# A gated attention and GEGLU kernel: wider staging, down weights split twice, late weight writes, attention in two stages

## The chip, the cores and the metric

The kernel runs on one core of a Trainium2 chip. The core has five engines that run in parallel, each through its own list of instructions in order: PE (TensorE, matrix products into PSUM banks), ACT (ScalarE), DVE (VectorE), POOL (GpSimd) and SP (SyncE, which here only issues DMAs). They meet at semaphores. DMAs are issued from the queues of SP, ACT and POOL. The metric is the device time of one execution in microseconds, and a kernel's figure is the median of its runs.

## The reference

For x of 2048 tokens and 512 channels, all in float32:

```
g   = sigmoid((x * gate_w).sum(-1))
a   = attention(x @ wqkv) @ wo      # 32 heads of 16 channels; a token sees itself and 7 earlier
                                    # ones at a distance of 2, 4, ... 14; softmax over these 8
b   = (gelu(x @ w_gate) * (x @ w_up)) @ w_down      # 1792 hidden channels
out = g * a + (1 - g) * b
```

Attention has a dilation of 2, so even tokens see even tokens alone, and odd ones odd ones alone.

## The kernel before, in words

**Precision.** A float32 factor is made into two parts of a type that PE multiplies at once: hi is the rounded value, lo the rest. A product is hi·hi + hi·lo + lo·hi, three matmuls of 128 x 128 by 128 x 512. Parts are made by `split` (L78): ACT copies hi, DVE subtracts to get lo. For the weights of the FFN another way is used: ACT writes the negated rounded value into the place of lo (scale -1), and a DMA from POOL's queue that adds (`accum_op`) puts the raw value on top; then ACT writes hi. That is one adding DMA and two ACT passes for each group.

**Order.** `par` is 0 for the 1024 even tokens, 1 for the odd ones; each is 8 tiles of 128 tokens (`jj`), in two blocks of 4. The order as written (L660 on) is: projection of even tokens, FFN 0 (even tokens), projection of odd tokens, attention output of even tokens (`finish(0)`), FFN 1 (odd tokens), attention output of odd tokens (`finish(1)`). The order as run is made at compile time by a scheduler with its own timing of each instruction; it keeps dependences and mixes the rest by priority, engine by engine. It also hands out tiles: a name such as "s" or "r" has a fixed number of buffers, and an instruction that wants one waits until the last user of that buffer is done. Every DMA issued by SP or ACT takes one of eight semaphores in turn, and waits on its queue until the DMA that had it before (eight places earlier) has landed; POOL's DMAs have eight of their own.

**Projections.** `project(par, cb)` makes keys and queries of half of the heads (cb 0 and 2) or values and the gate (cb 1). For each tile, 12 matmuls go to a PSUM bank (L179), and `take` (L185) copies it with ACT into a stage tile (L191) and stores it to HBM with two DMAs from ACT's queue (L194, L196). Stage tiles come from "s" (3 buffers) and "r" (2 buffers) in turn. The buffers "hh" and "hl" (6 each) hold parts elsewhere.

**Attention.** It is DVE's work. A unit is 128 channels (8 heads) of one parity; there are 8 units. `load_kq` loads k and q from HBM, `scores` multiplies and sums (L246, L248), `softmax` takes the maximum (L258), subtracts it (L260), lets ACT take exp (L262), sums (L263) and scales; `mix` loads v, multiplies and adds (L281 to L289), transposes and stores to HBM from SP's queue ("os", L296). `attention()` is a generator that yields after each few instructions; `pull` advances it from within projections and FFN, at a lower priority, so DVE does it between other work.

**FFN.** The 1792 hidden channels come in 14 chunks f. The gate and up weights of a chunk are fetched (`fetch`, POOL's queue), combined on DVE (`combine`, L360), and split into parts in two groups, g0 and g1 (`operands`, L365; two buffers each). `gate_up` makes gate and up for both blocks of tokens by a scheme of seven products in place of eight, each of 6 matmuls (L411), in three banks X_, W_ and Z_: after the first product b11, ACT copies X_ to W_ (L490); t1 into Z_, copied to p5 (L415); t2 into X_, copied to u2; a12 b21 into W_ gives the gate of block 0, and so on. The seventh product of f is issued within f + 1 (`fourth`). Gate goes through gelu (L506, L523), is multiplied by up (L424) and split (L426, L427; lo on DVE in FFN 0, on POOL in FFN 1). `down` (L439) multiplies the hidden part of two chunks by the down weights, two chunks after they are made; block 0 is kept in four banks, block 1 goes through tiles "rt" (L444, L463).

**Weights for the second FFN.** In FFN 0, `keep(f)` (L387) writes the finished parts of g0 and g1 (768 and 1024 KB) to HBM ("ws") and those of the down weights d (512 KB, "ds"), from SP's queue, as soon as they are made. In FFN 1 `operands` and `down_w` (L396) load them from there. In FFN 0 `down_w` makes d from the raw down weights, fetched to a tile "r" by `fetch_d` (POOL's queue).

**Attention output.** `finish(par)` loads the attention's result back ("os"), splits it (`channels`, L605), multiplies by wo into eight banks (L638), copies each bank to a stage tile (L650 on ACT, L648 on DVE; "s" and "r" for even tokens) and stores or adds it to out (L652, L654).

Of the kernel before, what the change touches and what calls it, by code (L numbers as in the profile page):

```python
# [15 lines left out]
P = 128  # L16
# [24 lines left out]
def tile_gated_mix(ctx: ExitStack, tc: tile.TileContext, xt, wqkv, wff, wo, out):  # L41
# [44 lines left out]
    KS, VS, QS, OS, WS, DS = {}, {}, {}, {}, {}, {}  # L86
# [84 lines left out]
    stages = iter(["s", "r", "s", "r", "s"] * 99)  # L171
# [13 lines left out]
    def take(ps, par, jj, hh, vals, eng=None):  # L185
        st = tl(next(stages))
        n = CU if vals else 512
        if eng:
            eng.tensor_copy(st[:, :n], ps[:, :n])
        else:  # L190
            nc.scalar.activation(st[:, :n], ps[:, :n], AF.Copy)  # L191
        two = st.rearrange("p (a c d) -> p a c d", a=2, c=2)
        dst = VS[par, hh] if vals else KS[par, hh]
        nc.scalar.dma_start(rows(dst[:, W:], jj), two[:, 0])  # L194
        if not vals:
            nc.scalar.dma_start(rows(QS[par, hh], jj), two[:, 1])  # L196
        elif not hh:
            nc.scalar.activation(z[:, par, jj:jj + 1], ps[:, CU:CU + 1], AF.Copy)

    def project(par, cb, bg=iter(())):  # L200
        for jj in range(NP):
# [9 lines left out]
            next(bg, None)  # L211
            pull(2.7)
# [9 lines left out]
    LG = {}  # L222
# [30 lines left out]

    def softmax(par, u):
        lg = LG[par, u]
        m = pool.tile([P, NP, UH], F32, name="m")
        by_w = lg.rearrange("p j w h -> p j h w")
        nc.vector.tensor_reduce(m, by_w, axis=AX.X, op=OP.max)  # L258
        yield 0.7
        nc.vector.tensor_tensor(lg, lg, m[:, :, None, :].to_broadcast([P, NP, W, UH]), op=OP.subtract)  # L260
        yield 0.7
        nc.scalar.activation(lg, lg, AF.Exp, scale=DH ** -0.5)  # L262
        nc.vector.tensor_reduce(m, by_w, axis=AX.X, op=OP.add)  # L263
        yield 0.7
        nc.vector.reciprocal(m, m)
        nc.vector.tensor_tensor(m, m, g[:, par, :, None].to_broadcast([P, NP, UH]), op=OP.mult)
        yield 0.4
# [38 lines left out]
    def attention():  # L306
        units = [(0, u) for u in range(NU)] + [(1, u) for u in range(NU)]
        yield from need(0, 0)
        load_kq(0, 0)
        yield from scores(0, 0)  # L310
        load_kq(0, 1)
        yield from scores(0, 1)
        yield from need(0, 1)
        for i, un in enumerate(units):
            if i > 1:
                yield from scores(*un)
            yield from softmax(*un)
            if 1 <= i < len(units) - 1:
                yield from need(units[i + 1][0], units[i + 1][1] // 2 * 2)
                load_kq(*units[i + 1])  # L320
            yield from mix(*un)
            done.add((*un, "o"))

# [19 lines left out]
    RAW, RD, KEEP = {}, {}, {}  # L343
# [43 lines left out]
    def keep(f):  # L387

        for i in range(2):
            w = KEEP.pop((f, i))  # L390
            WS[f, i] = dram.tile(list(w.shape), F32, name=f"ws{f}{i}")
            nc.sync.dma_start(WS[f, i], w.bitcast(F32))
        DS[f] = dram.tile([P, 1024], F32, name=f"ds{f}")
        nc.sync.dma_start(DS[f], WD[f].bitcast(F32))

    def down_w(par, f):  # L396
        d = WD[f] = tl("d", F32R)
        if par:
            nc.sync.dma_start(d.bitcast(F32), DS[f])
            return  # L400
# [3 lines left out]
        nc.scalar.activation(d[:, :512], rd, AF.Copy)  # L404

    def product(ps, a, w, start):
        for kc in range(2):
            ah, al = XOP[a, kc]
            wh, wl = (x[:, kc * P:(kc + 1) * P] for x in w)
            for n, (w_, a_) in enumerate(((wh, ah), (wh, al), (wl, ah))):  # L410
                nc.tensor.matmul(ps, w_, a_, start=(start and kc == 0 and n == 0), stop=(kc == 1 and n == 2), skip_group_check=True)  # L411
# [54 lines left out]
    def gate_up(par, f, steps):  # L466
# [23 lines left out]
        nc.scalar.activation(W_, X_, AF.Copy)  # L490
        Z_ = bank("p")
# [12 lines left out]
        product(W_, "a12", w["b21"], False)  # L504
# [31 lines left out]
    def ffn(par):  # L536
        XOP.update(((n, kc), X[par, blk, kc + k]) for n, blk, k in (("a11", 0, 0), ("a12", 0, 2), ("a22", 1, 2))
                   for kc in range(2))
        for f in range(FC):
            def more():  # L540
                if f + 1 < FC:
                    for i, _ in enumerate(operands(par, f + 1)):
                        if i == 1 and not par and f + 2 < FC:
                            fetch(f + 2)
                        if i == 2 and not par:
# [4 lines left out]
                if f + 1 == FC and not par:  # L550
                    yield from before()
                if not par:
# [7 lines left out]
            down_w(par, f)  # L560
# [53 lines left out]
    def need_o(par, u):  # L614
        pull(1e9, (par, u, "o"))

    def finish(par, oT, bg):
# [6 lines left out]
        for u in range(NU):  # L624
# [7 lines left out]
            for jj in range(NP) if u + 1 < NU else [*range(BT, NP), *range(BT)]:  # L632
# [12 lines left out]
                r = tl(("s", "rt" if par else "r")[jj % 2])  # L645
# [64 lines left out]
    project(1, 2)  # L710
    finish(0, {}, iter(()))
# [44 lines left out]
```

## Time and profile before

| what | value |
|---|---|
| median of 3 runs | 663.26 us (662.86 to 665.01) |
| the profiled execution | 665.45 us |
| its span, first to last instruction | 663.6 us |
| its mean granted PE clock | 0.984 of full speed |
| PE busy | 623.3 us, 94% |
| DVE busy | 518.5 us, 78% |
| ACT busy | 338.8 us, 51% |
| POOL busy | 136.1 us, 21% |
| bytes moved by DMA | 153.97 MB |

The profile names an instruction by its line, its engine and the tiles that it writes and reads. A row of PE counts matmuls; each is shown for about 0.4 us, but they overlap, so the time of a row of matmuls that follow each other is read from its start to the next row's start. "x <- y" in a list of waits says which engine sat idle and what released it. A q after an engine's name (SPq, ACTq) stands for its queue, where DMAs are issued. In a table of stretches the columns are the stretch, its length, PE's busy time with the number of matmuls, the granted clock, the busy share of the DMA engines, and GB/s. A row of the chain gives start, length and what the end of the kernel waited for at that time. Rows of DMA issues give the count, the size and the median time from issue to landing.

### The profile page before, as it was taken

The page shows a single profiled execution, that of the slowest core. Times are in us where ns is not written, and L with a number is a line of the kernel's source. Part 1 is how long each engine was busy: PE and PEld are TensorE (multiplying, and loading weights), DVE is VectorE, ACT ScalarE, POOL GpSimd, SP SyncE. Part 2 cuts the span into 40 slices and gives each one's busy share as a digit, 9 for nine tenths or more (in the row PEclk, how much of TensorE's full clock was granted, in tenths as well). Part 3 has the DMA queues.
Part 4 walks back from the last instruction along what each step waited for, and adds up shares of the span by engine and source line. Part 5 has one row for each costly group of instructions (what it writes and reads, how often), then busy time and mean ns, then how long its engine had stood idle before and what let it go on. Part 6 is the DMA issues. An engine that isn't in the chain of part 4 may idle for free.

```text
span 663.6 us, 8115 instructions
## 1 busy us (share of the span) xinstructions
PE 623.3 (94%) x2839; PEld 507.0 (76%) x2839; DVE 518.5 (78%) x567; ACT 338.8 (51%) x581; POOL 136.1 (21%) x161
## 2 busy tenths in 40 slices
PE   8999569998999998988999999799999999999997
PEld 7898447777778786776889888588878888878885
DVE  6939179988799789697984798988998999981241
ACT  5535057574667856558655422234445435444561
POOL 5012013132223222121110001342212222021100
PEclk9999979999999999998999999799999999999999
DMA  8688969999999999995669997954757472543113
GB/s 257 184 248 219 361 191 234 334 315 286 329 303 314 269 365 251 323 268 200 191 199 318 309 330 208 218 179 165 269 190 269 149 258 112 179 142 124 38 58 126
DMA packets 75336, 153.97 MB, mean 232 GB/s; under 512 B 7712, under 2 KB 43168, under 8 KB 71712
## 3 DMA queue, kind: packets, MB, share of 16 engines
q1 hardware_dynamic: 36000, 103.84, 43.9%
q0 software_dynamic: 13184, 37.04, 23.5%
q10 hardware_dynamic: 26112, 12.59, 6.5%
q8 instruction: 22, 0.36, 0.2%
q14 instruction: 18, 0.15, 0.1%
HBM read 80.76 MB, written 56.16 MB: 206 GB/s over the span
## 4 chain that ended last, share of the span: by engine, by line
PE 49%; DMA 26%; DVE 9%; issue 8%; ACT 5%; POOL 2%; ACTq 1%; SPq 0%; POOLq 0%; DVEq 0%
PE p L411 18%; DMA g<-raw 10%; PE p L179 7%; PE acc L179 7%; PE p L450 6%; PE acc L450 5%; PE p L638 3%; PE acc L638 3%; DMA raw<-wff 2%; DMA vs<-s 2%; DMA qs<-s 2%; DMA q<-qs 2%; DMA raw<-xt 2%; DVE prod L281 2%; DMA ws<-g 1%
## 5 line engine op out<-in xcount | busy, mean ns | idle before, releaser
L411 PE MATMUL p<-S,g 128*128 128x512 f32 x672 | 174.1, 400 | 18.9 <-ACT r L191 12.0
L411 PEld LDWEIGHTS p<-S,g 128*128 128x128 f32 x672 | 127.6, 191 | 51.6 <-ACT r L191 12.5
L411 PE MATMUL p<-A,g 128*128 128x512 f32 x504 | 133.4, 399 | 10.2 <-DMA g<-raw 6.2
L411 PEld LDWEIGHTS p<-A,g 128*128 128x128 f32 x504 | 95.0, 190 | 36.4 <-DMA g<-raw 9.4
L246 DVE TENSOR_TENSOR prod<-k,q 128x2048 f32<-128x2048 f32 x32 | 73.0, 2280 | 9.2 <-DMA q<-qs 9.0
L427 POOL TENSOR_TENSOR hl<-c,hh 128x512 fp32r<-128x512 f32 x28 | 45.4, 1622 | 160.4 <-ACT hh L426 117.1
L281 DVE TENSOR_TENSOR prod<-v,lg 128x2048 f32<-128x2048 f32 x32 | 75.0, 2343 | 0.8 <-DMA v<-vs 0.2
L450 PE MATMUL p<-d,hh 128*128 128x512 f32 x224 | 70.0, 401 | 4.9 <-ACT p L444 4.9
L248 DVE TENSOR_REDUCE lg<-prod 128x128 f32<-128x2048 f32 x32 | 73.0, 2281 | 0.3
L450 PE MATMUL acc<-d,hh 128*128 128x512 f32 x224 | 59.1, 395 | 0.0
L450 PEld LDWEIGHTS p<-d,hh 128*128 128x128 f32 x224 | 42.5, 191 | 16.3 <-ACT p L444 6.7
L426 ACT ACTIVATE hh<-c 128x512 fp32r<-128x512 f32 x56 | 35.2, 628 | 34.5 <-DVE c L424 34.1
L424 DVE TENSOR_TENSOR c<-c 128x512 f32<-128x512 f32 x56 | 38.4, 685 | 14.7 <-ACT c L523 14.1
L450 PEld LDWEIGHTS acc<-d,hh 128*128 128x128 f32 x224 | 42.0, 188 | 9.9 <-ACT hh L426 0.3
L463 ACT ACTIVATE rt<-p 128x512 f32<-128x512 f32 x48 | 28.0, 592 | 42.2 <-PE p L450 42.1
L420 DVE TENSOR_TENSOR c<-p,s 128x512 f32<-128x512 f32 x56 | 38.1, 682 | 13.5 <-PE p L411 13.1
L415 ACT ACTIVATE s<-p 128x512 f32<-128x512 f32 x56 | 32.8, 592 | 26.2 <-PE p L411 19.1
L450 PE MATMUL p<-d,hl 128*128 128x512 f32 x112 | 43.3, 401 | 0.0
L285 DVE TENSOR_TENSOR prod<-prod 128x1024 f32<-128x1024 f32 x32 | 39.5, 1235 | 0.3
L381 POOL DMA_DIRECT2D g<-raw x28 | 26.9, 1009 | 37.4 <-ACT g L380 32.3
L360 DVE TENSOR_TENSOR raw<-raw 128x256 f32<-128x256 f32 (+1 forms) x42 | 21.2, 507 | 16.9 <-DMA raw<-wff 11.6
L380 ACT ACTIVATE g<-raw 128x1024 fp32r<-128x1024 f32 (+1 forms) x28 | 26.6, 950 | 15.3 <-DVE raw L360 12.7
(150 smaller groups left out, 975.1 us busy)
## 6 DMA issues: line engine op xcount, KB each, us to landing
ws<-g SPq DMA_DIRECT2D x14, 1024.0 KB, 7.8
g<-ws SPq DMA_DIRECT2D x14, 1024.0 KB, 5.2
ws<-g SPq DMA_DIRECT2D x14, 768.0 KB, 8.6
g<-ws SPq DMA_DIRECT2D x14, 768.0 KB, 5.8
raw<-wff POOLq DMA_DIRECT2D x28, 256.0 KB, 8.1
g<-raw POOLq DMA_DIRECT2D x14, 512.0 KB, 10.8
ds<-d SPq DMA_DIRECT2D x14, 512.0 KB, 7.7
d<-ds SPq DMA_DIRECT2D x14, 512.0 KB, 6.0
```

Of the source, the lines that this page charges most:

```text
L179: nc.tensor.matmul(ps[:, :cn], a[:, t], w[:, c0:c0 + cn], start=(kc == 0 and n == 0), stop=(kc == KC - 1 and n == 2))
L246: nc.vector.tensor_tensor(prod, spans(k, jj), q[:, jj:jj + 2, None, :].to_broadcast([P, 2, W, UC]), op=OP.mult)
L248: nc.vector.tensor_reduce(lg[:, jj:jj + 2].rearrange("p j w h -> p (j w h)"), prod.rearrange("p j w (h d) -> p (j w h) d", d=DH), axis=AX. ...
L281: nc.vector.tensor_tensor(prod.rearrange("p j w (h d) -> p j w h d", d=DH), spans(v, jj).rearrange("p j w (h d) -> p j w h d", d=DH), lg[: ...
L285: nc.vector.tensor_tensor(prod[:, :, :4], prod[:, :, :4], prod[:, :, 4:], op=OP.add)
L411: nc.tensor.matmul(ps, w_, a_, start=(start and kc == 0 and n == 0), stop=(kc == 1 and n == 2), skip_group_check=True)
L420: nc.vector.tensor_tensor(c, ps, s, op=OP.add)
L424: nc.vector.tensor_tensor(ge, ge, up, op=OP.mult)
L426: nc.scalar.activation(hh_, ge, AF.Copy)
L427: eng.tensor_tensor(hl_, ge, hh_.bitcast(F32), op=OP.subtract)
L450: nc.tensor.matmul(pp, a[:, ts], w, start=(i == 0 and n == 0 and gr == 0), stop=(i == 1 and n == 2), skip_group_check=True)
L638: nc.tensor.matmul(pa, a, b, start=(not par and u == 0 and n == 0), stop=(u == NU - 1 and n == 2), skip_group_check=True)
```

## The change

Five edits go together.

1. The stage tiles of projections go round "s", "hh", "hl", "hh", "hl" in place of "s", "r" (15 buffers in place of 5). The attention output of even tokens is staged in "hh" and "hl" in place of "s" and "r".
2. The parts of the down weights are no longer written to HBM and read back. `down_w` makes them in both FFNs, from raw weights that `fetch_d` loads in both. It is called in the background work of a chunk; `fetch_d(0)` for FFN 1 comes after the last projection.
3. The writes "ws" of chunk f get an added wait: for the last matmul of the product a12 b21 of that chunk.
4. Attention is split into two stages. Of a unit, scores, maximum and subtraction come one unit ahead of sum, scaling and mix, and the load of the next unit's k and q comes between scores and maximum. The tile m has two buffers.
5. Exp is taken out of the generator: a list holds the units that wait for it, and `exps` issues them on ACT at fixed places (after a projection tile, after the copy X_ to W_ of a chunk, or when a result is needed), after having been passed over a number of times, and in the order as written.

```diff
-    stages = iter(["s", "r", "s", "r", "s"] * 99)
+    stages = iter(["s", "hh", "hl", "hh", "hl"] * 99)
...
     def take(ps, par, jj, hh, vals, eng=None):
-        st = tl(next(stages))
+        st = tl(next(stages))[:, :512]
...
             next(bg, None)
+            exps(5)
             pull(2.7)
...
+    def below_max(par, u):
+        lg = LG[par, u]
+        m = M[par, u] = pool.tile([P, NP, UH], F32, name="m", bufs=2)
+        nc.vector.tensor_reduce(m, lg.rearrange("p j w h -> p j h w"), axis=AX.X, op=OP.max)
+        yield 1.2
+        nc.vector.tensor_tensor(lg, lg, m[:, :, None, :].to_broadcast([P, NP, W, UH]), op=OP.subtract)
+        EXPS.append([lg, 0, (par, u)])
+        yield 0.7
+
+    def exps(n=-1):
+
+        for e in list(EXPS):
+            e[1] += 1
+            if e[1] > n:
+                EXPS.remove(e)
+                tc.keep_in_program_order(nc.scalar.activation(e[0], e[0], AF.Exp, scale=DH ** -0.5))
+                done.add((*e[2], "e"))
+
     def softmax(par, u):
-        lg = LG[par, u]
-        m = pool.tile([P, NP, UH], F32, name="m")
...
-        nc.scalar.activation(lg, lg, AF.Exp, scale=DH ** -0.5)
...
+        yield from need(par, u, "e")
+        lg, m = LG[par, u], M.pop((par, u))
...
     def attention():
-        units = [(0, u) for u in range(NU)] + [(1, u) for u in range(NU)]
...
+        def start(i):
+            if i < len(units):
+                yield from scores(*units[i])
+                if i + 1 != NU:
+                    yield from load(i + 1)
+                yield from below_max(*units[i])
+
+        yield from load(0)
+        yield from start(0)
         for i, un in enumerate(units):
-            if i > 1:
-                yield from scores(*un)
+            if i + 1 != NU:
+                yield from start(i + 1)
+            yield from need(un[0], 1)
             yield from softmax(*un)
...
             yield from mix(*un)
             done.add((*un, "o"))
+            if i + 1 == NU:
+                yield from load(NU)
+                yield from start(NU)
...
             WS[f, i] = dram.tile(list(w.shape), F32, name=f"ws{f}{i}")
-            nc.sync.dma_start(WS[f, i], w.bitcast(F32))
-        DS[f] = dram.tile([P, 1024], F32, name=f"ds{f}")
-        nc.sync.dma_start(DS[f], WD[f].bitcast(F32))
-
-    def down_w(par, f):
+            gate(nc.sync.dma_start(WS[f, i], w.bitcast(F32)), MARK[f])
+
+    def down_w(f):
         d = WD[f] = tl("d", F32R)
-        if par:
-            nc.sync.dma_start(d.bitcast(F32), DS[f])
-            return
         rd = RD.pop(f)
         nc.scalar.activation(d[:, 512:], rd, AF.Copy, scale=-1.0)
         nc.gpsimd.dma_start(d[:, 512:].bitcast(F32), rd, accum_op=OP.add)
         nc.scalar.activation(d[:, :512], rd, AF.Copy)
+
+    def gate(ins, other):
+
+        tc.add_manual_dep(ins.ins, other.ins.name, mybir.DependencyInfo(mybir.DependencyClass.Sync,
+                          mybir.DependencyReason.SCHED_ONLY), reason="pace")
...
         nc.scalar.activation(W_, X_, AF.Copy)
+        exps(1)
...
-        product(W_, "a12", w["b21"], False)
+        MARK[f] = product(W_, "a12", w["b21"], False)
...
-                        if i == 2 and not par:
+                        if i == (0 if par else 2):
                             fetch_d(f + 1)
...
                 if f + 1 == FC and not par:
                     yield from before()
+                down_w(f)
+                yield
                 if not par:
                     keep(f)
...
-            down_w(par, f)
...
     def need_o(par, u):
-        pull(1e9, (par, u, "o"))
+        while (par, u, "o") not in done:
+            exps()
+            pull(1e9, (par, u, "o"))
...
-                r = tl(("s", "rt" if par else "r")[jj % 2])
+                r = tl((("s", "rt") if par else ("hh", "hl"))[jj % 2])[:, :512]
...
     project(1, 2)
+    fetch_d(0)
     finish(0, {}, iter(()))
```

## The prediction, made before the run

> **What bounds the kernel now.** I read the page's engine shares and 40 slices first, then TensorE (PE) over five stretches, then what PE waited for, then the chain and ScalarE's (ACT's) timeline where the largest gap lies, and the DMA issues last.
>
> ```profile
> PE 623.3 (94%) x2839; PEld 507.0 (76%) x2839; DVE 518.5 (78%) x567; ACT 338.8 (51%) x581; POOL 136.1 (21%) x161
> PEclk9999979999999999998999999799999999999999
> DMA  8688969999999999995669997954757472543113
> GB/s 257 184 248 219 361 191 234 334 315 286 329 303 314 269 365 251 323 268 200 191 199 318 309 330 208 218 179 165 269 190 269 149 258 112 179 142 124 38 58 126
> ```
> ```profile
> core 0: us, PE busy (x), PEclk, DMA share, GB/s
> 74.30:116.90 42.60, 27.82 (x109) 0.88 0.86 252
> 116.90:321.50 204.60, 190.94 (x803) 0.99 0.94 290
> 321.50:413.70 92.20, 92.20 (x494) 1.00 0.85 272
> 413.70:431.00 17.30, 12.95 (x44) 0.81 0.94 213
> 431.00:637.00 206.00, 204.76 (x882) 1.00 0.49 171
> ```
> ```profile
> PE p L411 <- ACT r L191: 12.0, 1, 12.0
> PE p L411 <- DMA g<-raw: 6.2, 6, 1.7
> PE p L411 <- ACT s L415: 5.2, 3, 3.4
> PE p L450 <- ACT p L444: 4.9, 3, 2.3
> PE p L411 <- DVE c L420: 3.9, 3, 1.6
> ```
> ```profile
> 62.40 7.73 DMA ws<-g
> 70.15 15.16 DMA qs<-s
> 100.47 5.06 DMA d<-r
> 105.53 2.88 DMA r<-wff
> 108.41 7.99 DMA g<-raw
> 461.60 5.59 PE p L411 x24
> ```
> ```profile
> 70.62 0.60 ACT L191 ACTIVATE r<-acc 128x512 f32<-128x512 f32 x1 [4.93 <-DMA ws<-g]
> 81.41 0.60 ACT L191 ACTIVATE s<-acc 128x512 f32<-128x512 f32 x1 [10.19 <-DMA qs<-s]
> 425.41 2.93 PE L411 MATMUL p<-S,g 128*128 128x512 f32 x6 [3.42 <-ACT s L415]
> ```
> ```profile
> ws<-g SPq DMA_DIRECT2D x14, 768.0 KB, 8.6
> ```
>
> What to see. PE is the bound: the chain has 24 matmuls in 5.59 us, 0.233 us each. A chunk f of the hidden channels needs 42 product and 24 down matmuls, 66 x 0.233 = 15.4 us. Length minus matmuls x 0.233 gives what each stretch loses: 17.2, 17.5, none (its matmuls are partly narrower, PE is busy throughout), 7.0 and 0.5; together 42.2. No part of this change removes a matmul, so these losses are all that it can win.
>
> The first loss is the end of the attention projections. ACT copies a projection to SBUF and issues its store to HBM itself. In the program every DMA of SyncE (SP) or ACT waits for the one eight places before it, since they share eight semaphores. So ACT's stores stood behind the weight writes ws and the v, k and q loads: one store was in flight for 15.16 us, and ACT waited 4.93 and 10.19 us while PE stood 12.0. The second loss is FFN 0 with DMA engines 94% busy. The third, at 413.7, is a copy that wants a stage tile "s" while the store of the attention output still holds it.
>
> **The change, part by part.** The sum is made against the profiled execution: 665.45 us, span 663.6 and 1.85 outside, 2.19 above the median of 663.26.
>
> A, projections and start of FFN 0 (74.3 to 116.9, loses 17.2). The rotation of stage tiles grows from 5 buffers to 15, and writes ws of f = 0 wait for that chunk's product a12 b21, about 81 us. Three writes (2.9 MB) that went out at 49.1, 62.4 and 64.9 leave this stage. Not all lanes clear: v, k and q loads of unit 0 and 1 still take places among the eight, and ACT's stores of tiles 4 to 6 wait for k and q (median 6.9 and 7.5 us; they can go out about 65, when DVE has left the old k). They end about 73 to 75, in time for the last projection at 74.3. So the 12.0 goes. What is late next is a chain on down weights. The new order puts both parts of d for f = 0 and 1 (whose loads now go first on POOL's queue, at the very start) before the chunk, and d for f = 2 and 3, ahead of the copy u2 of chunk 0, on ACT. Their loads wait on POOL for the d accumulations to land. From about 75.5: accumulation 5.8 (lowest of 14, median 7.9), issue 0.5, load 4.3 (row at 95.24; lowest 3.4, median 7.3), three ACT passes 1.9, copy 0.6: 88.6. PE can run 36 matmuls without u2, to 74.3 + 8.4 = 82.7, so it stands 6; with the lowest values 4, with the medians 11. Behind the same chain stands, on POOL, the accumulation of the first g weights of f = 2 (two loads ahead of it wait for d to land, 5.8 more): issued about 95.5, landing 8.0 later (row at 108.41) at 103.5, wanted at 100: 3.5, between 0 and 7. With 1.5 of slow clock (six matmuls at 0.42 after the old gap) the stage loses 11 in place of 17.2: minus 6. Ends: 4 left (minus 13), 17 left (nothing).
> By the Trainium skill (DMA: Bandwidth & Descriptors, Anatomy of one DMA) one transfer takes 2.0 us plus bytes / 436e3, 2.6 for these 256 KB; that is an estimate, and by it the chain would end under 82.7, nothing would stand there, and the sum would be 6 lower. The trace has 7.9 and 7.3 as medians, so I don't take it.
>
> B, FFN 0 (204.6 us, 803 / 66 = 12.2 chunks of 16.8). The writes ds leave: 14 x 0.524 MB. SP's queue moved 103.84 MB in 43.9% of the span, 2.8 us of all engines per MB, so 20.6 us; the three moved writes bring back 8.1. Net 12.5, about 1.0 per chunk. DMA work per chunk falls from 0.94 x 16.8 = 15.8 to 14.8, under PE's 15.4, so the six waits on g<-raw (6.2) should fall to 2. The 4.9 behind ACT L444 and 2.7 of the 3.9 behind DVE L420 stay, they are queue orders. Against it: writing late makes a loop. Product a12 b21 of f lets SP write both groups (SP also has attention's os stores and loads in that queue, which now wait behind the gated writes); ACT's first pass over the next g of the same buffer waits for the landing, and stands ahead of the copy W_ for chunk f + 1, without which the next a12 b21 can't run. Price of a round: landing L, lo and hi 1.7, hh, rt and W_ 1.8, every second round four d passes of 2.5, product 1.4: L + 6.2 on the mean. With the median 8.4 (4.2 to 19.0) this is 14.6, just under 15.4; six of 28 writes took over 11.4. I put 1 on it: 17.5 - 4.2 + 1 = 14; half of the DVE waits going with DVE's 17 us of exp wait moved earlier, I take 12.5. Minus 5, between minus 12.5 (5 left, the small waits alone) and plus 6.5 (24 left).
>
> C, output of even tokens (loses 7.0). Its stage tiles become hh and hl, so 3.42 and the slow clock behind it (2.93 for six matmuls, 1.5 too many, and four more at 0.42, 0.8) go: 5.7. ACT now has two d pairs and their loads ahead of the last attention channels; from 391 that chain takes 10 to 18, and PE wants them at 408: nothing to 3. I take 0.7. Minus 5 (minus 6.5 to minus 1).
>
> D, FFN 1 (loses 0.5). 28 ACT passes of 0.62 are 17.4 us on an engine about half busy, 28 POOL issues 22 us on one that is idle most of the time, and the reads of ds (7.3 MB) leave a DMA half idle. A d pair ahead of W_ costs 1.2 where PE is closely fed. Since d is used two chunks later, I take 0.5; 0 to 4.
>
> E, start. Two loads of 256 KB now go first, beside the x and w loads that PE waits for. The first slice moved 257 GB/s, so 0.52 MB costs up to 2.0. I take 1.
>
> F, at nothing: attention in two stages. DVE's waits for exp were 22.4, of which 17.0 is the wait of A; DVE is not PE's limit where attention runs out (its last units end about 40 us before FFN 1 does, and A to C take back about 15 of that). Exp now has a fixed place on ACT; its table loads stay 16 in the program. The projections of odd tokens lose nothing before, so more tiles bring nothing.
>
> Sum: -6 - 5 - 5 + 0.5 + 1 = -14.5; 665.45 - 14.5 = 650.95 as a profiled execution, less 2.19: **649**.
>
> **Rivals.** (1) Chains at unloaded latency: fewer bytes in flight make d, r and g land at their lowest rows. A leaves 5, B 8, C 0.5: -12 - 9.5 - 6.5 + 1 = -27, 636. For: 12.5 us of DMA work go. Against: PE starts FFN 0 earlier, so work per us hardly falls. (2) The loop takes FFN 0's gain: B + 4, the rest as forecast, -5.5: 658. (3) Slower: the loop binds throughout. B must lose 9.5 more than before, 27 in 12.2 chunks, 17.6 a chunk, so L over 11.4 on the mean. At L = 12.4: 18.6, B + 21.5, sum + 12: 675. For it: L reached 12 to 19 beside other writes, and a late os store holds a gated write. Against: the median of 8.4, and a late PE empties the DMA queue. (4) More tiles don't matter since the eight semaphores bind, and k and q loads replace ws in front of ACT's stores: A and B stay as they are, C gives 5, D and E cost 2 each: 662.
>
> By the same skill (TensorE: Matmul & The Clock Gate, HAM oscillation) PE gaps over about 3.4 us bring a slow clock. Here 3.42 did, and one of 2.3 at 311 too (PEclk has an 8 there). That speaks against the change: one gap of 12 turned into two pays twice, 1.4 more than I count.
>
> **How the numbers follow.** Forecast (640 to 656) 0.50, rival 1 0.20, rival 2 0.15, rival 3 0.11, rival 4 0.04. 0.3% of 663 is 2 us, about what a measurement tells from no change. Faster 0.85, same 0.04 (rival 4), slower 0.11. The range leaves out most of rival 3 and the tail of rival 1, 0.2 together: 636 to 662. The ends of all terms would give 631 and 675.
>
> **What would show it.** A: no PE gap of 12 at the end of the projections, a smaller one before the third product of f = 0 that ends on ACT's copy behind d<-r and r<-wff, and one before f = 2. B: 803 matmuls in less than 200 us, waits on g<-raw under 3, ACT's first pass over g released by DMA ws<-g. C: no wait for out<-s. D: FFN 1 at 15.4 per chunk. Wrong if ws<-g lands in over 11 us and PE waits behind ACT in each chunk of FFN 0, or if ACT still waits 10 us for stores of the projections.

## The result, and the profile after

The changed kernel takes 674.86 us (median of 4 runs, 673.27 to 676.5), the kernel before 664.13 in the runs beside it. The ratio is 1.016, 95% interval 1.0125 to 1.0193: slower, where 649 (636 to 662) was forecast. The profiled execution took 676.5 us with a span of 674.7, 11.1 more than the span of before. The profile's engine shares and slices:

```profile
PE 631.6 (94%) x2839; PEld 512.1 (76%) x2839; DVE 517.1 (77%) x567; ACT 351.7 (52%) x609; POOL 161.7 (24%) x189
...
DMA  8597889789889988986669997955748465535123
```

Against before, ACT has 28 more instructions (581 there) and POOL 28 more (161): the second making of the down weights. The DMA digits of FFN 0 (from the eighth on) are mostly 8 and 9, where before had nines. So the change does what it says. The stretches, cut at the same counts of matmuls as before (stretch, length, PE's busy time and matmuls, clock, DMA share, GB/s):

```profile
0.00:8.26 8.26, 4.40 (x34) 0.98 0.67 206
77.20:118.60 41.40, 30.52 (x108) 0.88 0.87 249
118.60:326.50 207.90, 193.09 (x803) 0.98 0.87 252
...
396.00:436.30 40.30, 35.45 (x141) 0.92 0.91 233
436.30:648.50 212.20, 207.39 (x883) 0.99 0.53 167
```

For the last two the rows of before, cut alike, are:

```profile
391.20:431.10 39.90, 35.55 (x141) 0.92 0.87 242
431.10:637.00 205.90, 204.66 (x882) 1.00 0.49 171
```

Length less matmuls x 0.233 again gives what a stretch loses. The last column but one is the changed kernel without edits 4 and 5; the last is the changed kernel with one word less, which lets exp move on ACT. Both are shown below.

| lost, us | before | forecast | changed | without 4, 5 | exp free |
|---|---|---|---|---|---|
| start, beyond the 5.8 of before (E) | 0 | 1 | 2.5 | 2.3 | 2.5 |
| end of projections, start of FFN 0 (A) | 17.2 | 11 | 16.2 | 11.0 | 14.0 |
| FFN 0 (B) | 17.5 | 12.5 | 20.8 | 10.2 | 10.6 |
| output of even tokens (C) | 7.0 | 2 | 7.4 | 7.1 | 1.4 |
| FFN 1 (D) | 0.5 | 1 | 6.5 | 1.7 | 2.7 |
| sum | 42.2 | 27.5 | 53.4 | 32.3 | 31.2 |
| median of the runs, us | 664 | 649 | 674.9 | 658.2 | 655.3 |

The sums differ by 11.2, as the spans do. What PE waited for in the changed kernel (engine, line, tile and releaser; us in total, times, longest):

```profile
PE p L434 <- DVE c L444: 7.1, 4, 2.7
PE p L434 <- ACT p L514: 6.1, 3, 4.0
PE p L666 <- ACT hh L82: 4.9, 1, 4.9
...
PE p L434 <- DMA g<-raw: 3.8, 2, 2.9
PE p L474 <- POOL hl L451: 3.1, 2, 2.3
```

The 12.0 us gap behind a stage tile is gone, as forecast, and of the 6.2 on g<-raw in FFN 0 there is 0.9 left (2.9 of the 3.8 lie at its start, before f = 2); other waits stand in their places. Four of them can be followed in the timeline.

**Start of FFN 0.** The copies of the last projections ran on ACT from 78.3 to 85.6, where the stores ahead of them were expected to be done by 75: ACT still waited for its own stores (5.76 us), then came exp, two copies and four d passes, and W_ (L514), for which PE waited 4.03, behind them.

```profile
78.29 0.60 ACT L191 ACTIVATE hh<-p 128x512 f32<-128x512 f32 x1 [5.76 <-DMA ks<-s]
81.41 0.63 ACT L270 ACTIVATE lg<-lg 128x512 f32<-128x512 f32 x1 [0.96 <-DVE raw L383]
82.43 0.62 ACT L420 ACTIVATE d<-r 128x512 fp32r<-128x512 f32 x1
85.54 0.59 ACT L514 ACTIVATE p<-p 128x512 f32<-128x512 f32 x1
86.19 2.79 PE L434 MATMUL p<-S,g 128*128 128x512 f32 x6 [4.03 <-ACT p L514]
```

**FFN 0.** POOL loads r only after d<-r has landed, g<-raw and the raw weights queue behind it, DVE sits idle for them, and the additions c are late:

```profile
193.97 0.57 POOL L377 DMA_DIRECT2D r<-wff  x1 [1.31 <-DMA d<-r]
200.49 0.73 POOL L372 DMA_DIRECT2D raw<-wff  x1 [5.96 <-DMA g<-raw]
204.47 0.69 DVE L383 TENSOR_TENSOR raw<-raw 128x512 f32<-128x512 f32 x1 [4.99 <-DMA raw<-wff]
215.62 2.55 PE L434 MATMUL p<-A,g 128*128 128x512 f32 x6 [2.73 <-DVE c L444]
```

**Output of even tokens.** Exp is held at its place on ACT and waits 3.14 us for DVE's subtraction. The copy, four d passes and another copy follow, and only then the parts of the attention output, which PE waits for:

```profile
396.89 0.63 ACT L270 ACTIVATE lg<-lg 128x512 f32<-128x512 f32 x1 [3.14 <-DVE lg L260]
399.59 0.61 ACT L422 ACTIVATE d<-r 128x512 fp32r<-128x512 f32 x1
400.59 0.62 ACT L82 ACTIVATE hh<-raw 128x512 fp32r<-128x512 f32 x1
401.26 2.07 PE L666 MATMUL p<-g,hh 128*128 128x512 f32 x4 [4.86 <-ACT hh L82]
```

**FFN 1.** The load r waits on POOL for d<-r, and the hl that PE wants stands behind it:

```profile
490.42 0.55 POOL L377 DMA_DIRECT2D r<-wff  x1 [4.97 <-DMA d<-r]
490.99 5.83 POOL L451 TENSOR_TENSOR hl<-c,hh 128x512 fp32r<-128x512 f32 x2
494.64 0.50 PE L474 MATMUL p<-d,hl 128*128 128x512 f32 x1 [2.29 <-POOL hl L451]
```

### The profile page after: what moved, and what is told of

It reads as the page before. It is cut to its first block, busy times and chain, and to the rows that moved or that the text cites. A ratio compares the mean times of both kernels' runs of the same rounds, so it can differ in the third digit from the quotient of the medians.

```text
span 674.7 us, 8120 instructions
## 1 busy us (share of the span) xinstructions
PE 631.6 (94%) x2839; PEld 512.1 (76%) x2839; DVE 517.1 (77%) x567; ACT 351.7 (52%) x609; POOL 161.7 (24%) x189
## 5 line engine op out<-in xcount | busy, mean ns | idle before, releaser
L434 PE MATMUL p<-A,g 128*128 128x512 f32 x504 | 136.9, 410 | 11.9 <-DVE c L444 7.1
L434 PEld LDWEIGHTS p<-A,g 128*128 128x128 f32 x504 | 97.9, 196 | 38.8 <-DVE c L444 10.0
L294 DVE TENSOR_TENSOR prod<-v,lg 128x2048 f32<-128x2048 f32 x32 | 76.5, 2391 | 1.1 <-DMA v<-vs 0.8
L451 POOL TENSOR_TENSOR hl<-c,hh 128x512 fp32r<-128x512 f32 x28 | 52.1, 1861 | 104.4 <-ACT hh L450 97.7
L421 POOL DMA_DIRECT2D d<-r x28 | 24.8, 885 | 100.2 <-ACT d L420 88.3
L404 POOL DMA_DIRECT2D g<-raw x28 | 24.4, 885 | 71.1 <-ACT g L403 52.5
```

Of the source, the lines that this page charges most:

```text
L294: nc.vector.tensor_tensor(prod.rearrange("p j w (h d) -> p j w h d", d=DH), spans(v, jj).rearrange("p j w (h d) -> p j w h d", d=DH), lg[: ...
L434: mm = nc.tensor.matmul(ps, w_, a_, start=(start and kc == 0 and n == 0), stop=(kc == 1 and n == 2), skip_group_check=True)
L451: eng.tensor_tensor(hl_, ge, hh_.bitcast(F32), op=OP.subtract)
```

## The experiments

Theory 1 at the outset was the chain of the down weights seen in these rows; its rivals were the late writes (the prediction's third rival) and the attention edits. Every kernel's order is made anew by the scheduler, so an edit can also move what it doesn't touch. Ratios are to the kernel before in runs beside it.

### One edit alone

Edit 2 (down weights made twice) on the kernel before:

```diff
-        DS[f] = dram.tile([P, 1024], F32, name=f"ds{f}")
-        nc.sync.dma_start(DS[f], WD[f].bitcast(F32))
...
+                down_w(f)
+                yield
```

> The kernel before with edit 2 alone: the parts of the down weights d are made in both FFNs, from raw weights that POOL loads, and neither written nor read back. Theory 1 (the chain of d costs what the change lost: POOL loads r of a chunk only after the adding DMA d<-r of an earlier one has landed, and everything behind that load on POOL's queue, g<-raw and hl, waits too; and ACT's two passes per d stand in front of copies that PE wants): 12 to 16 us slower than before (about 678), made of 2 at the start (x loads beside the two first loads of r), 3 to 5 at the attention output of even tokens, 5 to 6 in FFN 1 with waits of PE for POOL's hl, 2 or more at the start of FFN 0. Theory 2 (the late weight writes cost it): between 8 us faster and 2 slower, since the writes ds leave FFN 0. Theory 3 (the two-stage attention costs it): within 3 us of before.

Measured: 676.9 us, 1.018 (1.014 to 1.022). The trace is of the quickest of its six runs (670.5, the others up to 678.7), so it shows 5 of the 13 us: 6 in FFN 1 and 4 in FFN 0, while the projections' end gained 3. The 6 in FFN 1 is the size that theory 1 gave, but not its reason: PE's waits for POOL's hl are 0.9 us there, those for DVE's c 3.0. The start lost 0.2, not 2, and the attention output nothing: those two parts of theory 1 fail here.

Edit 3 (late writes) on the kernel before:

```diff
-            nc.sync.dma_start(WS[f, i], w.bitcast(F32))
+            gate(nc.sync.dma_start(WS[f, i], w.bitcast(F32)), MARK[f])
```

> The kernel before with edit 3 alone: writes ws of chunk f wait for the product a12 b21 of f. Theory 1: the 12 us gap at the end of the projections shrinks, because three weight writes leave it, and FFN 0 hardly moves: 4 to 8 us faster (about 657). Theory 2: the loop through the landing of the write slows FFN 0: 5 us slower or more (over 669), PE waiting behind ACT's first pass over g in most chunks. Theory 3: within 3 us of before, or faster as in theory 1.

Measured: 665.5, 1.005 (1.002 to 1.007). The projections' end gained 5.8 (36.7 us in place of 42.5), and FFN 0 lost 4.8 (209.4 in place of 204.6). Neither of the first two theories: gain and loss cancel, and 2.0 us more than before is within the 3 of theory 3.

Edits 4 and 5 (attention) on the kernel before:

```diff
-        nc.scalar.activation(lg, lg, AF.Exp, scale=DH ** -0.5)
+        EXPS.append([lg, 0, (par, u)])
...
+                tc.keep_in_program_order(nc.scalar.activation(e[0], e[0], AF.Exp, scale=DH ** -0.5))
```

> The kernel before with edits 4 and 5 alone: attention in two stages, exp at fixed places on ACT. Theory 1: within 2 us of before (DVE does the same work). Theory 2: the same. Theory 3 (DVE's long attention operations now stand in front of the additions c that PE waits for, and exp in front of copies): 5 to 8 us slower (about 670), with PE's waits for DVE c at 6 us or more in FFN 0, as in the changed kernel, where they were 3.9 over the whole of before.

Measured: 675.3, 1.018 (1.0155 to 1.020). A step that was costed at nothing costs about 12 us alone, more than any of the theories gave. In FFN 0 PE's waits for DVE c were 2.4, where theory 3 wanted 6; those for g<-raw were 8.8.

Edit 1 (stage tiles) on the kernel before:

```diff
-    stages = iter(["s", "r", "s", "r", "s"] * 99)
+    stages = iter(["s", "hh", "hl", "hh", "hl"] * 99)
...
-                r = tl(("s", "rt" if par else "r")[jj % 2])
+                r = tl((("s", "rt") if par else ("hh", "hl"))[jj % 2])[:, :512]
```

> The kernel before with edit 1 alone: stage tiles s, hh, hl for the projections, hh and hl for the attention output of even tokens. All three theories: the wait of PE for a stage tile at the attention output of even tokens goes (3.4 and the slow clock behind it), 3 to 6 us. Theory 1 says of the 12 us gap at the end of the projections that it stays at 8 or more, since the weight writes still hold the eight semaphores of ACT's and SP's DMAs: 3 to 7 us faster in all (about 659). If the tiles were what held ACT, it goes as well: 14 to 18 us faster (about 648).

Measured: 661.6, 0.997 (0.995 to 0.999). The output of even tokens lost 1.0 (33.9 us with 141 matmuls) in place of 7.0: term C, and more. The 12 us gap became 6.0. But the first projection was held up by 2.3, which had been expected of edit 2: nothing else uses the tiles r at the start any more, so the loads into them go out first (at 1.3 and 2.0 us; at 89.9 and 95.2 before), and PE waits for the second part of x. Its first matmuls:

```profile
4.32 1.60 PE L179 MATMUL p<-g,A 128*128 128x512 f32 x3
8.05 0.50 PE L179 MATMUL p<-g,A 128*128 128x512 f32 x1 [2.13 <-DVE A L80]
```

Alone, the four came to 25 us more; together they cost 11. So they don't add up, and the next runs leave one out.

### One edit left out

Without edit 2:

```diff
-                down_w(f)
-                yield
...
+            down_w(par, f)
```

> The changed kernel without edit 2: down weights by way of HBM again. Alone on the kernel before, edits 1 to 5 gave -2 (stage tiles), +13 (down weights), +2 (late writes) and +12 (two-stage attention with placed exp), 25 together, where all at once cost 11. Theory 1 (each edit's own mechanism stands in the changed kernel): 9 to 13 us faster than the changed kernel, about 663, made of 4 to 5 at the attention output of even tokens (no d passes on ACT ahead of it), 4 to 5 in FFN 1 (no PE wait for POOL's hl) and the rest in FFN 0. Theory 2 (FFN 0 and FFN 1 have one shared limit, DVE's queue, which any of the edits upsets as much): under 5 us faster, 670 or more.

Measured: 673.8, 1.014 (1.011 to 1.016): 1 us gained, not 9 to 13. Of theory 1 the parts in FFN 1 (2.8 less) and at the attention output (6.3 less) come off, and FFN 0 takes them back (213.1 us, 5 more). What edit 2 costs there it also earns elsewhere.

Without edits 4 and 5:

```diff
-            exps(5)
...
-        exps(1)
...
+        nc.scalar.activation(lg, lg, AF.Exp, scale=DH ** -0.5)
```

> The changed kernel without edits 4 and 5: attention in one stage, exp where it was. Theory 1: 8 to 12 us faster than the changed kernel, about 665, with fewer waits of PE for DVE's additions c in both FFNs. Theory 2: under 5 us faster, since edit 2 alone brought PE's waits for DVE c to 12.6 us without touching attention: 670 or more.

Measured: 658.2, 0.990 (0.988 to 0.992): 16.7 us quicker than the changed kernel, and quicker than before. Its stretches, in the order A, B, C, D:

```profile
77.20:113.40 36.20, 29.04 (x108) 0.91 0.94 269
113.40:310.70 197.30, 189.40 (x803) 0.99 0.90 265
380.30:420.30 40.00, 34.72 (x141) 0.91 0.87 218
420.30:627.70 207.40, 205.64 (x883) 1.00 0.54 174
```

A and B lose 11.0 and 10.2, against forecasts of 11 and 12.5. The attention edits are what turned the gain into a loss.

Without edit 3:

```diff
-            gate(nc.sync.dma_start(WS[f, i], w.bitcast(F32)), MARK[f])
+            nc.sync.dma_start(WS[f, i], w.bitcast(F32))
```

> The changed kernel without edit 3: weight writes as soon as the parts are made. If the late writes bind FFN 0 by their loop (ACT waited 20.7 us for the landing of ws there): 5 us faster or more, under 670. If they only move waits from one engine to another: within 3 us of the changed kernel, with the 12 us gap at the end of the projections back in part, so that the stretch from the projections' end to the end of FFN 0 stays at 244 to 250 us as in all kernels so far.

Measured: 668.3, 1.006 (1.004 to 1.008), 6.5 quicker than the changed kernel. The stretch from the projections' end through FFN 0 took 245 us: the 12 us gap is back by half (6.2), and FFN 0 is nearly the same, 207.3. The trace, of its quickest run, is 12 us shorter, 3 to 4.5 each at the projections' end, the attention output and FFN 1. The time is the one that the first theory gave, but FFN 0 isn't where it came from: the late writes are not what makes FFN 0 long in the changed kernel.

A control: only the prices with which attention's instructions are spread, on the kernel before (the first of three is shown).

```diff
         nc.vector.tensor_reduce(m, by_w, axis=AX.X, op=OP.max)
-        yield 0.7
+        yield 1.2
```

> The kernel before, with only three of the prices that softmax reports to its caller changed as edit 4 has them (0.7 to 1.2 for the maximum and the sum, 0.4 to 0.8 for the scaling). No instruction is added or taken away; they are laid into DVE's order at other places. If the two-stage order itself is what costs: within 2 us of before (662 to 666). If the place of attention's instructions among DVE's additions is what matters, and any shift of it can cost: 4 us or more away from before, to either side.

Measured: 663.2, 0.9985 (0.996 to 1.001). So a shift of attention's instructions costs nothing by itself, at least not this one; the edit to exp or the new order is left.

### Exp: its place, its lateness, its pin

Edit 5 undone, edit 4 kept:

```diff
-        EXPS.append([lg, 0, (par, u)])
+        nc.scalar.activation(lg, lg, AF.Exp, scale=DH ** -0.5)
+        done.add((par, u, "e"))
```

> The changed kernel with edit 5 undone and edit 4 kept: exp is issued by the attention generator itself, right after the subtraction, as before; the two stages stay. Without edits 4 and 5 the changed kernel took 658.2, with both 674.9. If the places of exp on ACT are what costs (attention stands until the next chunk's place for exp, and DVE fills its order with other work that is not ready on the chip): 662 or less. If the two-stage order of attention costs: 671 or more. In between, both.

Measured: 655.9, 0.987 (0.983 to 0.991). All 19 us go with edit 5; the two stages cost nothing (658.2 without them).

Passed over less often:

```diff
-            exps(5)
+            exps(0)
...
-        exps(1)
+        exps(0)
```

> The changed kernel with exp issued at the first of its places after the subtraction (passed over 0 times, in place of 5 at projection tiles and 1 at chunks); order as written kept. The changed kernel took 674.9, with exp in the generator 655.9. There, exp ran 4 to 49 us after its subtraction in the changed kernel and 2 to 6 us in the other. Theory delay (the late exp makes the second stage of a unit late and puts it among other work of DVE): most of the 19 comes back, 663 or less. Theory pin (exp, held in order on ACT, makes the copies behind it wait for DVE's subtraction, 3.1 us ahead of the attention output): 670 or more, since the same pins stand, nearer to the subtraction.

Not held in order:

```diff
-                tc.keep_in_program_order(nc.scalar.activation(e[0], e[0], AF.Exp, scale=DH ** -0.5))
+                nc.scalar.activation(e[0], e[0], AF.Exp, scale=DH ** -0.5)
```

> The changed kernel with exp at the same places of the program but free to be laid elsewhere on ACT (it need not follow what was written before it). Theory delay: exp is still written one chunk late and what waits for it too: 669 or more. Theory pin: most of the 19 comes back, 663 or less.

Measured: 661.4 (0.997, 0.994 to 1.000) with the earlier places, 655.3 (0.985, 0.980 to 0.989) without the pin. The last unit's subtraction (DVE) and exp (ACT) in the changed kernel:

```profile
545.91 0.67 DVE L260 TENSOR_TENSOR lg<-lg,m 128x512 f32<-128x512 f32 x1
594.93 0.63 ACT L270 ACTIVATE lg<-lg 128x512 f32<-128x512 f32 x1
```

and with exp free:

```profile
517.83 0.67 DVE L260 TENSOR_TENSOR lg<-lg,m 128x512 f32<-128x512 f32 x1
521.02 0.63 ACT L270 ACTIVATE lg<-lg 128x512 f32<-128x512 f32 x1
```

Summed over the 8 units, the time from the end of the subtraction to the start of exp is 136 us in the changed kernel, 69 with the earlier places, 18 with exp free and 16 with exp in the generator; the times are 674.9, 661.4, 655.3 and 655.9. Theory delay was right about the first run and theory pin about the second. They are one mechanism: the pin is what makes exp late (freed, the scheduler moves it up to its subtraction), and in these four kernels, which differ in the handling of exp alone, the cost goes with the lateness. Elsewhere it doesn't by itself: without edit 3 the sum is 129 us at 668.3, and with DVE relieved (below) 172 at 663.1. The stretches with exp free:

```profile
77.30:116.50 39.20, 29.05 (x108) 0.91 0.91 264
116.50:314.20 197.70, 189.21 (x803) 0.99 0.90 265
383.80:418.30 34.50, 32.78 (x142) 1.00 0.95 240
418.30:626.50 208.20, 206.06 (x882) 0.99 0.53 169
```

Against the changed kernel 2.2 come back at the start of FFN 0, 10.2 in FFN 0, 6.0 at the attention output and 3.8 in FFN 1. The 6.0 is seen in rows: ACT stands at the pinned exp, the one of the eight that ran as soon as its subtraction was done. A pin isn't the only way to lose it. In the run without edits 4 and 5 the scheduler had laid exp at the same spot, and DVE's subtraction was late there too:

```profile
381.16 0.63 ACT L262 ACTIVATE lg<-lg 128x512 f32<-128x512 f32 x1 [3.31 <-DVE lg L260]
385.97 2.07 PE L640 MATMUL p<-g,hh 128*128 128x512 f32 x4 [5.28 <-ACT hh L82]
```

Of the 10.2 in FFN 0, 6.4 are waits of PE (14.8 against 8.4 with exp free, those for DVE c 5.8 against 3.4) and 3.9 its busy time (193.09 against 189.21, at a granted clock of 0.98 against 0.99). How a late exp leads to these waits, and to those of FFN 1, isn't shown: that it costs there is shown by the runs, not by a chain of waits.

### Is DVE the bound of FFN 0?

In the kernels up to here FFN 0 was mostly longer the more DVE sat idle there. So DVE was relieved, in the changed kernel and in the one before:

```diff
-            nc.vector.tensor_tensor(prod[:, :, :4], prod[:, :, :4], prod[:, :, 4:], op=OP.add)
+            nc.vector.tensor_tensor(prod[:, :, :4, :8], prod[:, :, :4, :8], prod[:, :, 4:, :8], op=OP.add)
```

> The changed kernel with DVE relieved: the first of the additions over the products of v, 32 instructions of 1.26 us, adds 8 of 128 channels only (this part of the sum over the window is left out for the others). Theory A (in FFN 0 DVE is the bound: the stretch of 207.9 us holds 192 us of DVE work, and its length in all kernels so far goes with DVE's idle time there): some 22 of the 32 lie in FFN 0, 20 to 25 us of DVE work less; FFN 0 gets 10 us shorter or more (its matmuls alone take 187), and the kernel takes 662 or less. Theory B (DVE only passes on what DMA landings and ACT's order make late): within 4 us of the changed kernel, 671 or more.

> The same relief of DVE in the kernel before (the same part of the sum left out). Theory A: FFN 0, 204.6 us there with 188 of DVE work, gets 8 us shorter or more, the kernel takes 655 or less. Theory B, which is how the prediction read the profile (PE waits for the adding DMAs g<-raw and for queue orders on ACT): within 4 us of before, 660 or more.

Measured: 663.1 (0.999, 0.996 to 1.002) for the changed kernel, 662.0 (0.9975, 0.994 to 1.001) for the one before. The row of DVE in FFN 0 before, and then with the relief:

```profile
117.00:321.60 204.60, 176.13 (x210) 0.99 0.94 290
```
```profile
118.60:322.90 204.30, 170.58 (x218) 1.00 0.95 292
```

DVE has 30 us less to do in all, but only 6 to 8 less in FFN 0, since attention's other work moved there: the test is weaker than planned. (The 192 and 188 us of the expectations are durations, which overlap; the busy time is 176 in both.) Before, 5.6 us less of DVE changed FFN 0 by 0.3 us, so theory A fails there, and DVE's idle time was a companion. The changed kernel lies between its two theories: 11.8 us quicker, and FFN 0 went from 207.9 to 201.3 with 7.5 us less of DVE, though exp was later still (172 us in sum). There DVE's order is part of the bound, and a late exp costs less where DVE has less to do.

### Edits 2 and 3 belong together

The same kernels with edit 2 taken away, first without edits 4 and 5, then with the two stages and exp in the generator:

```diff
+        DS[f] = dram.tile([P, 1024], F32, name=f"ds{f}")
+        nc.sync.dma_start(DS[f], WD[f].bitcast(F32))
```

> The changed kernel without edits 4 and 5 (658.2) and without edit 2 (down weights by way of HBM again): stage tiles and late writes alone. Theory 1 (what edit 2 costs there is what the trace of the run without 4 and 5 shows: 6 at the attention output, 2 in FFN 1; that the writes ds leave FFN 0 gains little): 6 to 9 us faster than 658.2, 649 to 652. Theory 2, the prediction's term B (the writes ds are 20.6 us of DMA time in FFN 0, and FFN 0 gained 7 by their absence): within 3 us of 658 or slower.

> As the run before, with the two-stage order (edit 4) and exp in the generator, that is the changed kernel with edits 2 and 5 undone. Exp in the generator gave 655.9 with edit 2. If what edit 2 costs at the attention output and in FFN 1 is cost here too: there the lost time was 2.2 and 4.2, so 2 to 5 us faster, 651 to 654; if the writes ds cost FFN 0 more than that: 658 or more.

And with edit 2, but without edit 3 (exp in the generator):

```diff
-            gate(nc.sync.dma_start(WS[f, i], w.bitcast(F32)), MARK[f])
+            nc.sync.dma_start(WS[f, i], w.bitcast(F32))
```

> The changed kernel with exp in the generator (655.9) and without the late writes (edit 3 undone). Without edit 2, the kernels with late writes were at 668 and 674, and edit 2 alone without late writes at 676.9. Theory pair (the two belong together: with the writes ds gone a late ws lands in 4 to 7 us and costs no wait, and only late writes clear the eight semaphores at the projections' end): 8 us slower or more, 664 or over, the stretch from the last projections to 66 matmuls into FFN 0 at 39 us or more (36.0 with late writes). Theory 2 (late writes give nothing, edit 2 does it all): within 3 us of 655.9.

| stage tiles, and | late writes | d made twice | us | ratio (95%) |
|---|---|---|---|---|
| nothing else | no | no | 661.6 | 0.997 (0.995 to 0.999) |
| one stage | yes | no | 673.6 | 1.013 (1.010 to 1.016) |
| one stage | yes | yes | 658.2 | 0.990 (0.988 to 0.992) |
| two stages, exp in generator | yes | no | 668.0 | 1.007 (1.005 to 1.009) |
| two stages, exp in generator | no | yes | 663.4 | 0.9985 (0.9955 to 1.0015) |
| two stages, exp in generator | yes | yes | 655.9 | 0.987 (0.983 to 0.991) |

With late writes, edit 2 is worth 15 and 12 us; with edit 2, late writes are worth 7.5. Without edit 2 late writes lose 12 beside the new stage tiles (2 beside the old ones, edit 3 alone). Theory 1 of the run without edit 2 is wrong: what edit 2 costs at the output and in FFN 1 is small beside what it gives FFN 0. FFN 0 without edit 2 and with it (both with late writes):

```profile
118.80:329.30 210.50, 193.82 (x803) 0.98 0.90 271
```
```profile
113.40:310.70 197.30, 189.40 (x803) 0.99 0.90 265
```

The stretch moved 57.0 MB in one and 52.3 in the other; by B's 2.8 us per MB the 4.7 are 13 us of DMA work, near to the difference of 13.2. That isn't proof: the DMA share is 0.90 in both, and the kernel before moved more, 59.3 MB, in 204.6 us. Why late writes cost so much beside the writes ds is therefore open. A late write also lands later beside them. DMA issues, median us to landing, without edit 2:

```profile
ws<-g SPq DMA_DIRECT2D x14, 1024.0 KB, 9.1
ws<-g SPq DMA_DIRECT2D x14, 768.0 KB, 6.4
```

and with it:

```profile
ws<-g SPq DMA_DIRECT2D x14, 1024.0 KB, 6.9
ws<-g SPq DMA_DIRECT2D x14, 768.0 KB, 4.2
```

With edit 2 and early writes the stretch at the projections' end took 38.8 us (109 matmuls) against 35.9 (108), just under the 39 expected, as 663.4 is just under the 664, and FFN 0 205.1 against 201.7.

### The start, and a quicker kernel

The first loads of r held back in both FFNs, without edits 4 and 5:

```diff
-        nc.gpsimd.dma_start(RD[f], wff[f, :, 1024:])
+        ins = nc.gpsimd.dma_start(RD[f], wff[f, :, 1024:])
+        if f < 2:
+            gate(ins, MARK["d"])
```

> The changed kernel without edits 4 and 5 (658.2), and with the first two loads of raw down weights of each FFN held back: in FFN 0 until the last matmul of the projection of values, in FFN 1 until half of the attention output of even tokens. If these loads and the four passes behind them are what the start (2.5) and the attention output (5.4 and the slow clock behind it, 2) lost: 6 to 9 us faster, 650 to 652. If not: within 2 us of 658.

Measured: 669.1, 1.006 (1.003 to 1.0095), with eleven runs from 663.8 to 671.8 and one at 675.8. The start was repaired (34 matmuls in 5.5 us), but the rest lost 13: FFN 0 7.3 more, FFN 1 3 more, the attention output unchanged. Why FFN 0 pays for it isn't settled.

Held back less long and in FFN 0 alone, with exp in the generator:

```diff
+        if f < 2 and f not in MARK:
+            gate(ins, MARK["x"])
```

> The changed kernel with exp in the generator, and with the first two loads of raw down weights held back until the first projection's bank is done (about 17 us), so that they don't run beside the loads of x. If these two loads are what delays the first projection by 2.3 to 2.7 us in all kernels with the new stage tiles: that time comes back, 653, with no wait of PE for the second part of x beyond 0.6. If the order of everything behind shifts as well, the sum can go elsewhere, as with the loads held until 37 us, where the start was repaired and FFN 0 lost 7.

Measured: 654.0, 0.982 (0.978 to 0.987): the quickest kernel here, 10 us less than before and 21 less than the changed one. The first 34 matmuls are done in 6.01 us again, so the two loads are the cause of the 2.5. Its margin over 655.9 is within the runs' spread, and the attention output took back 4.5 in the profiled run, its slowest (657.0).

```profile
0.00:6.01 6.01, 4.43 (x34) 1.00 0.59 167
383.10:422.30 39.20, 35.53 (x142) 0.91 0.89 226
```

## Why the prediction was wrong

**F failed.** "Attention in two stages" was costed "at nothing", and of exp it said only that it "now has a fixed place on ACT". The number of table loads, which did stay at 16, was taken for the whole price. The runs put 16.7 us on edits 4 and 5 and 19 on edit 5, all by the pin. What had to be priced is when the place comes: exp, passed over once, stands behind a later chunk's W_ copy, up to 48 us after the subtraction, and where DVE is late ACT stands there and waits. None of the four rivals and neither sign of being wrong had exp in it: the writes ws landed in 5.8 and 8.4 us (medians by size), not over 11, and ACT's longest wait for a store of the projections was 5.8, not 10.

**A was right in size, not in its steps.** Without edits 4 and 5 the stretch loses 11.0, as forecast (14.0 with exp free), and the wait for g<-raw of f = 2 is 2.8 (3.5 forecast). But the gap stands at the W_ copy behind four d passes (2.0 there, 4.0 in the changed kernel) with 1.0 and 1.3 before u2, not 6 before u2, and in the changed kernel ACT still waited for its stores at 78, the lanes not being clear by 75. The chain on d itself was quicker than costed: d<-r 3.3, load 4.0. By the Trainium skill (DMA: Bandwidth & Descriptors, Anatomy of one DMA) such a load of 256 KB would take 2.6, an estimate; in the changed kernel the median is 5.3 for r and 5.7 for d<-r, so the trace differs. With 2.6 for both, the prediction's own sum gives 83.7, not an end under 82.7.

**B came out, a little small, with its mechanism seen in part.** Waits for g<-raw fell as forecast, and FFN 0 loses 10.2 (12.5 forecast), both without edits 4 and 5. The DMA work fell from 192 us (204.6 x 0.94) to 178, 14 where 12.5 was forecast; that this work sets the stretch's length is not shown. The third rival's 675 was met by accident: its loop did not bind, since the writes landed in 7.0 on the mean, where it needed over 11.4, and ACT waited for ws<-g 30 us in the quick kernel without edits 4 and 5 and 21 in the slow one.

**C was right but for what stands ahead on ACT.** Forecast 2 lost, 1.0 with the stage tiles alone, 1.4 with exp free, but 7.4 with exp pinned and 7.1 without edits 4 and 5: it depends on how late ACT is done with what stands ahead of the output's first parts. In these two that is exp, waiting 3.1 and 3.3 us for DVE's subtraction, and four d passes of 2.2 and 2.6 us together. Neither decides alone: with exp free the d passes stand there too and PE waits 1.7, in the quickest kernel 3.7; without edits 2, 4 and 5 there are no d passes, and behind an exp that waits 3.5 PE waits 4.9. The prediction put the d passes ahead of the last parts and exp nowhere, and bounded what stands there by 3; the kernel with the pin and the one without differ by 6.0 here.

**D was mis-sized**, 0.5 for a measured 1.7 to 2.7, and 6.5 with exp pinned. Of these 6.5, waits for POOL's hl behind an r load are 3.1; without edits 4 and 5 such waits are 1.0, and with exp free there are none, so the rest of D isn't traced. The prediction saw in A that loads of r wait on POOL for d<-r and hold g<-raw; in D it only counted POOL's issues. **E** was 2.5, not 1, and belongs to edit 1.

With exp free the spans differ by 10.7 in place of the forecast's 14.5, and 655.3 lies in the forecast's own range of 640 to 656. That is in part luck: A and E lose 4.5 more than forecast and D 1.7 more, B and C 2.5 less.

## What to carry to other kernels

Price an instruction that is held at a place of an in-order queue by its distance from what it needs and from who needs it, not by its length: one ACTIVATE of 0.63 us, eight times, cost 19 us. An edit can lose alone and gain beside another: late writes took the kernel with new stage tiles from 661.6 to 673.6, and with the down weights made twice to 658.2, so measure such edits in pairs before dropping one. When an edit frees a tile, look at which loads go out early because of it.

## What was unexpected of the hardware

PE's slow matmuls (0.42 us in place of 0.233) follow shorter gaps than 3.4 us. Over the twenty profiles, from 30 us on, a gap taken as the time between two starts less 0.233, and the next 24 matmuls looked at (slow is 0.36 to 0.5 from start to start): all 23 gaps above 4 us were followed by 5 to 15 slow ones, 33 of 38 gaps between 3 and 4, 31 of 50 between 2 and 3, and 16 of 186 between 0.6 and 2. With no other gap over 0.6 among the 24 matmuls before and behind, these are 15 of 15, 19 of 24, 24 of 38 and 3 of 116, the last with one slow matmul each. The granted clock says the same. Over the 6 us behind a gap of 2.0 to 3.4 it is 0.51 to 0.76 in the 42 cases of 63 with slow matmuls, and 1.00 in the others. One of the 42 stands in FFN 1 of the changed kernel; the second row is six matmuls that take 2.6 us to the next row's start, where 1.4 is usual:

```profile
494.64 0.50 PE L474 MATMUL p<-d,hl 128*128 128x512 f32 x1 [2.29 <-POOL hl L451]
496.70 2.76 PE L434 MATMUL p<-A,g 128*128 128x512 f32 x6
```

The Trainium skill (TensorE: Matmul & The Clock Gate, HAM oscillation) has about 3.4 us as the bound; here gaps of 2.0 to 3.4 pay as well, in 42 of 63 cases.
